# Reading four of the 32 float64 weight pieces through the expert weights' pool

## The chip, the cores and the metric

One NeuronCore of one Trainium2 chip runs the whole program. The metric is the time of one execution on the device in microseconds (us). The engines named below are TensorE (PE, matmuls; PEld is its weight load), VectorE (DVE), ScalarE (ACT), GpSimd (POOL) and SyncE (SP), which here only issues DMA transfers.

## What is computed

Block-local attention gives 1536 tokens of 512 features. A router assigns every token to one of 8 experts (192 tokens each), and each expert is a two-layer MLP in float32. Its output goes through one last MLP whose weights come in float64:

```python
def _moe_ref(x, w_gate, w1, w2):
    ...
    for e in range(E):                      # 8 experts, 192 tokens each
        mask = assigned == e
        h = np.maximum(x[mask] @ w1[e], 0.0)      # 512 -> 1024
        out[mask] = h @ w2[e]                     # 1024 -> 512
    return out.astype(np.float32)

def _moe2_ref(x, w_in, w_out):
    h = x @ w_in                                  # 512 -> 2048, w_in float64
    r = np.maximum(h, 0.0)
    g = r * r
    return (g @ w_out).astype(np.float32)         # 2048 -> 512, w_out float64
```

## The kernel before, in words

Three stages follow each other: attention and its routing scores, then the eight experts (with the rest of the routing woven in), then the last MLP. All instructions are issued in an order that the Python code fixes; each engine runs its own list in order.

**Experts.** Expert `ph` reads four tiles of 128x4x512 floats (1 MB, two DMA transfers each) from a pool `m_w` of eight buffers that are used in turn: tiles 0 and 1 are w1, tiles 2 and 3 are w2. `w_next` keeps a list `wl` of the tiles still to be read and reads the next when the buffer eight places back in the order will be free. SP issues them (L925); before each it loads the expert's number from `ei`, and for tile 1 also a flag `fl` that is set behind the gathers of the tokens. TensorE's matmuls are those of L956 (first layer, 64 for an expert) and L973 (second layer, 64). ScalarE takes the first layer's results out of PSUM (`ht`, L961), ScalarE and VectorE those of the second (`yhi` L979, `ylo` L980).

**Conversion of the float64 weights.** The two matrices are cut into 32 pieces of 128x512 doubles (512 KB). Piece i belongs to quarter i//8; the first four pieces of a quarter are rows of `w_in`, the last four rows of `w_out`. A piece is read into a tile `raw` of the pool `m_stg`, which has two buffers, by `conv_load` (SP, L625). `conv_stream` then turns it into two float32r tiles, the rounded value and the remainder, in four VectorE instructions (L640, L644 and L650 build the float32 bits; L647 subtracts the rounded value of the piece before) and one copy on ScalarE (L643). One call of `conv_step` is one VectorE instruction, so a piece is four steps, 128 in all. Quarter 0 goes to tiles `w2a`, quarter 1 to `w2b`, quarters 2 and 3 to buffers of the expert pool `m_w` that are free by then. The two `raw` buffers alternate: piece i+2 is read when L650 of piece i is done.

**What decides when a piece is converted.** While the experts run, `conv_idle` is called after every piece of TensorE work. It keeps estimated clocks of the engines and issues conversion steps where VectorE is estimated to be idle and the piece is estimated to have landed. In the last MLP a fixed number takes over: six steps after each unit.

**The last MLP.** There are 48 units (3 groups of 512 tokens, 16 blocks of 128 hidden features). A *hidden unit* `hmm(i)` is 12 matmuls of L1065; ScalarE applies the relu (L1068), VectorE squares it (L1069), ScalarE rounds it (L1073) and VectorE makes the remainder (L1074). An *output unit* `omm(i)` is 12 matmuls of L1091 that read both. TensorE's order is hmm(0), hmm(1), hmm(2), omm(0), hmm(3), omm(1) and so on: omm(i) comes after hmm(i+2). Unit i needs quarter (i mod 16)//4 of the weights.

```python
    for i in range(len(seq) + LAG):
        if i < len(seq):
            while ndone[0] < min(len(todo), 8 * (i // 4) + 8):
                conv_step()
            hmm(i)
        if i >= LAG:
            omm(i - LAG)
        conv_step(SF if i < 16 else 1)          # SF = 6
```

Of the kernel before, what the change touches and what calls it, by code (L numbers as in the profile page):

```python
# [9 lines left out]
F32 = mybir.dt.float32  # L10
# [3 lines left out]
I32 = mybir.dt.int32  # L14
# [7 lines left out]
N, DM, E, F, FF = 1536, 512, 8, 1024, 2048  # L22
# [573 lines left out]
def moe(tc, nc, R0, x_dram, m_dram, L9, w1, w2, win, wout, out, identf, identb, dbg=None):  # L596
    ctx = ExitStack()
    const = ctx.enter_context(tc.tile_pool(name="m_const", bufs=1))
    wp = ctx.enter_context(tc.tile_pool(name="m_w", bufs=8))
# [11 lines left out]
    stg = ctx.enter_context(tc.tile_pool(name="m_stg", bufs=2))  # L611
    W, w2b = {}, []
    todo = [(q, io, k) for q in range(4) for io in range(2) for k in range(4)]
    raws = {}

    nload, nfree, eager = [0], [2], [True]

    def conv_load(i):
        q, io, k = todo[i]
        raw = raws[i] = stg.tile([128, 512, 2], I32, name="raw")  # L620
        if io == 0:
            src = win[128 * k:128 * k + 128, 512 * q:512 * q + 512]
        else:
            src = wout[512 * q + 128 * k:512 * q + 128 * k + 128, :]
        nc.sync.dma_start(raw.rearrange("p a b -> p (a b)"), src.bitcast(I32))  # L625
        nload[0] = i + 1

    def conv_stream():

        prev = None  # L630
        for i, (q, io, k) in enumerate(todo):
            if k == 0:
                pool, nm = (w2a, "w2a") if q == 0 else (w2b[0], "w2b") if q == 1 else (wp, "w8")
                W[io, q] = [pool.tile([128, 4, 512], F32R, name=nm) for _ in range(2)]
            while i not in raws:
                conv_load(nload[0])
            raw = raws.pop(i)
            f = stg.tile([128, 512], F32, name="f")
            fi = f.bitcast(I32)
            nc.vector.tensor_scalar(fi, raw[:, :, 1], 3, 0x3FFFFFF8, op0=OP.logical_shift_left, op1=OP.bitwise_and)  # L640
            yield
            if prev:
                nc.scalar.activation(prev[1], prev[0], AF.Copy)  # L643
            nc.vector.scalar_tensor_tensor(fi, raw[:, :, 0], 29, fi, op0=OP.logical_shift_right, op1=OP.bitwise_or)  # L644
            yield
            if prev:
                nc.vector.tensor_tensor(prev[2], prev[0], prev[1].bitcast(F32), op=OP.subtract)  # L647
                ndone[0] = i
                yield
            nc.vector.scalar_tensor_tensor(fi, raw[:, :, 1], -0x40000000, fi, op0=OP.bitwise_and, op1=OP.bitwise_or)  # L650
            nfree[0] = i + 3
            if not eager[0] and i + 2 < len(todo):
                conv_load(i + 2)
            prev = f, W[io, q][0][:, k, :], W[io, q][1][:, k, :]
            yield
        nc.scalar.activation(prev[1], prev[0], AF.Copy)
        nc.vector.tensor_tensor(prev[2], prev[0], prev[1].bitcast(F32), op=OP.subtract)
        ndone[0] = len(todo)

    ndone, nstep, CST = [0], [0], conv_stream()  # L660

    def conv_step(n=1):
        for _ in range(n):
            if w2b or nstep[0] < 32:
                nstep[0] += 1
                next(CST, None)
# [9 lines left out]
    st = {}  # L676
    T = Clock()
# [11 lines left out]
    def routing():  # L689
        tm_at = T.v(0.1)  # L690
        for ph in range(E):
# [70 lines left out]
            else:  # L762
# [10 lines left out]
                T.v(0.4, T.pe + 0.25)  # L773
            d["ei"] = ei
            w_next()

            os_ = rp.tile([128, NBLK], F32, name="os")
# [113 lines left out]
    def t_gather(ph):  # L891

        d = st[ph]
        xa = d["xa"] = f1.tile([128, DM], F32, name="xa")
        xb = d["xb"] = f1.tile([128, DM], F32, name="xb")[0:64, :]
        nc.gpsimd.indirect_dma_start(out=xa, out_offset=None, in_=x_dram,
                                     in_offset=bass.IndirectOffsetOnAxis(ap=sci[:, d["ka"]:d["ka"] + 1], axis=0))
        nc.gpsimd.indirect_dma_start(out=xb, out_offset=None, in_=x_dram,
                                     in_offset=bass.IndirectOffsetOnAxis(ap=d["ib"][:, :1], axis=0))
        fl = d["fl"] = rp.tile([1, 1], I32, name="fl", bufs=4)  # L900
        nc.gpsimd.memset(fl, 0)
        out = T.g(2.3, max(d["ix_at"], T.pe) + 0.1)
        d["tx"] = out + 3.0 + 0.5 * min(max(T.dma - out, 0.0), 3.0)
        T.d(1.0, out)
        w_next()

    wl, done, used = [(ph, i) for ph in range(E) for i in range(4)], [-1], [8]

    def w_next():

        while wl and ("tx" if wl[0][1] else "ei") in st.get(wl[0][0], ()) and 4 * wl[0][0] + wl[0][1] < used[0]:
            w_load(*wl.pop(0))

    def w_load(ph, i):

        d = st[ph]
        eng = nc.sync
        if i == 1:
            eng.value_load(d["fl"][0:1, 0:1], min_val=0, max_val=N - 1)
        r = eng.value_load(d["ei"][0:1, 0:1], min_val=0, max_val=E - 1)  # L920
        s1 = w1[bass.ds(r, 1)].rearrange("o (k p) f -> p (o k) f", p=128)
        s2 = w2[bass.ds(r, 1)].rearrange("o (k p) f -> p (o k) f", p=128)
        t = wp.tile([128, 4, 512], F32, name="w8")
        for k in (0, 2):
            eng.dma_start(t[:, k:k + 2, :], s1[:, k:k + 2, 512 * i:512 * i + 512] if i < 2 else  # L925
                          s2[:, 4 * i - 8 + k:4 * i - 6 + k, :])
        d.setdefault("w", []).append(t)
        T.d(3.1, T.pe)
# [17 lines left out]
    def expert(ph):  # L946
# [3 lines left out]
        for f0 in (0, 2, 4, 6):  # L950
            ps = p_f.tile([128, 2, 256], F32, name="ph", bufs=3)
            for j in range(2):
                f = f0 + j
                w = d["w"][f // 4]
                for k in range(4):
                    nc.tensor.matmul(ps[:, j, 0:CAP], w[:, k, 128 * (f % 4):128 * (f % 4) + 128], d["xt"][:, k, :],  # L956
                                     start=(k == 0), stop=(k == 3), skip_group_check=True)
                    T.p(0.325)
                    if k < 3 or j == 0:
                        yield  # L960
            nc.scalar.activation(d["ht"][:, f0:f0 + 2, :], ps[:, :, 0:CAP], AF.Relu)  # L961
            T.a(0.5, T.pe + 0.2)
            if f0 in (2, 6):
                used[0] += 1
                w_next()
            yield
# [20 lines left out]
    R = routing()  # L987
    nx, ng = [0], [0]
    rt, cur = next(R), None

    freed, landed = {}, {}

    def conv_idle():

        while nload[0] < min(nfree[0], len(todo)) and freed[nload[0]] <= T.pe:
            landed[nload[0]] = T.d(1.6, T.pe) + 2.8
            conv_load(nload[0])
        while (R is None or len(st) >= done[0] + 4) and T.dve < T.pe - 0.3 and landed.get(nfree[0] - 2, 1e9) <= T.pe:
            n0, f0 = nstep[0], nfree[0]
            conv_step()  # L1000
            if nstep[0] == n0:
                return
            T.v(0.7, T.pe - 0.7)
            if nfree[0] > f0:
                freed[nfree[0] - 1] = T.dve + 1.0

    for i in range(2):
        landed[i] = 5.0
        conv_load(i)
    while done[0] < E - 1:  # L1010
        gathers()
        ways = []
# [12 lines left out]
        if way == 0:  # L1025
            rt = next(R, None)
            if rt is None:
                R = None
# [15 lines left out]
            w2b.append(ctx.enter_context(tc.tile_pool(name="m_w2b", bufs=4, side="right", reuse_waits="tile")))  # L1044
        conv_idle()
    eager[0] = False
    while nload[0] < min(nfree[0], len(todo)):
        conv_load(nload[0])
    p_g = ctx.enter_context(tc.tile_pool(name="m_pg", bufs=4, space=PSUM))


# [70 lines left out]
@with_exitstack  # L1122
def kernel(ctx: ExitStack, tc: tile.TileContext, q, k, v, wg, w1, w2, win, wout, out):
    nc = tc.nc
    const = ctx.enter_context(tc.tile_pool(name="const", bufs=1))
    dram = ctx.enter_context(tc.tile_pool(name="dram", bufs=1, space=bass.MemoryType.DRAM))
    identf = const.tile([128, 128], F32, name="identf")
    make_identity(nc, identf)
    identb = const.tile([128, 128], BF, name="identb")
    nc.vector.tensor_copy(identb, identf)  # L1130
    L9 = const.tile([128, NBLK, E + 1], F32, name="L9")
    x_dram = dram.tile([N, DM], F32, name="x_dram")
    m_dram = [dram.tile([N], F32, name=f"m_dram{i}") for i in range(E)]
    ctx.enter_context(tc.manual_schedule())
    route = Route(tc, nc, L9, identf)
    with ExitStack() as actx:
        attention(actx, tc, nc, q, k, v, wg, x_dram, L9, identf, identb, route)
    moe(tc, nc, route, x_dram, m_dram, L9, w1, w2, win, wout, out, identf, identb)
# [29 lines left out]
```

## Time and profile before

| | us |
|---|---|
| median of 3 runs | 592.31 (591.49 to 594.31) |
| the profiled execution | 592.71 |
| its span, first to last instruction | 590.5 |
| PE busy | 570.6 (97%) |
| DVE busy | 342.6 (58%) |
| ACT busy | 195.9 (33%) |
| mean granted TensorE clock | 0.994 |

The busy time of PE is modelled from pipelined matmuls, so 97% does not mean that there is no time to be had in 3%: a matmul at half clock is busy too. The stages are: attention up to about 84 us, experts and routing up to 312, the last MLP from 312.3 to the end. Rows of a timeline give the start and the duration of an instruction and, in brackets, the idle time of its engine before it and what ended that idle time.

### The profile page before, as it was taken

What the parts mean: (1) busy time and instruction counts of PE and PEld (TensorE: products, weight loads), DVE (VectorE), ACT (ScalarE), POOL (GpSimd) and SP (SyncE); (2) the same over time, 40 slices, a digit from 0 to 9 for tenths busy, and PEclk for the clock granted to TensorE, in tenths of its full rate; (3) what the DMA queues carried; (4) which work ended last, traced back from release to release, by engine and by line L of the source; (5) the groups of instructions that cost most, each with busy time, mean ns of one, the idle gap of its engine ahead of it and who ended that gap; (6) DMA issues with size and microseconds to landing.
All of it is one profiled execution on the core that took longest, in us unless ns stands there. A gap on an engine that the chain in (4) does not pass through costs nothing.

```text
span 590.5 us, 10523 instructions
## 1 busy us (share of the span) xinstructions
PE 570.6 (97%) x4131; PEld 475.8 (81%) x4131; DVE 342.6 (58%) x773; ACT 195.9 (33%) x421; POOL 81.2 (14%) x136
## 2 busy tenths in 40 slices
PE   6999998999999999999999998899999999999996
PEld 4777874699898988999998876678888888888884
DVE  5875788887878889634656777772322222322222
ACT  4887862241331314022223333232322222222221
POOL 6663301110401202110000000000300000300002
PEclk9999999999999999999999999899999999999999
DMA  8997224645185474598342433410100000100001
GB/s 223 263 193 142 70 75 143 240 156 193 64 285 202 137 284 140 202 360 309 108 142 73 148 137 108 147 67 2 71 2 0 1 0 1 71 1 0 1 0 71
DMA packets 55392, 71.33 MB, mean 121 GB/s; under 512 B 21296, under 2 KB 32560, under 8 KB 55344
## 3 DMA queue, kind: packets, MB, share of 16 engines
q1 hardware_dynamic: 53360, 64.38, 34.7%
q0 software_dynamic: 1984, 6.29, 3.2%
q8 instruction: 32, 0.52, 0.4%
q14 instruction: 16, 0.13, 0.1%
HBM read 64.37 MB, written 6.29 MB: 120 GB/s over the span
## 4 chain that ended last, share of the span: by engine, by line
PE 65%; issue 14%; DVE 10%; DMA 6%; ACT 2%; POOL 2%; SPq 0%; POOLq 0%; DVEq 0%; ACTq 0%
PE ph L956 15%; PE ph L973 14%; PE pg L1065 9%; PE ph L1091 7%; PE px L1091 2%; PE cnt L582 2%; PE O L284 2%; DMA raw<-in_moe_w_out_dram 2%; PE S L250 2%; PE T L270 2%; DMA raw<-in_moe_w_in_dram 2%; DVE G L570 2%; PE T L193 1%; DVE f L650 1%; DMA rawq<-in_q_dram 1%
## 5 line engine op out<-in xcount | busy, mean ns | idle before, releaser
L956 PE MATMUL ph<-xt,w 128*128 128x192 f32 x512 | 91.1, 331 | 0.0
L973 PE MATMUL ph<-ht,w 128*128 128x192 f32 x512 | 89.3, 329 | 0.0
L570 DVE TENSOR_SCALAR G<-mrow,m 128x1536 bf16<-128x1536 f32 (+4 forms) x108 | 84.9, 839 | 7.5 <-PE cnt L582 3.9
L973 PEld LDWEIGHTS ph<-ht,w 128*128 128x128 f32 x512 | 82.9, 190 | 3.1 <-issue 2.9
L956 PEld LDWEIGHTS ph<-xt,w 128*128 128x128 f32 x512 | 82.5, 190 | 3.4 <-issue 2.7
L1065 PE MATMUL pg<-yhi,w 128*128 128x512 f32 x192 | 59.8, 392 | 2.1 <-ACT w L643 1.6
L1069 DVE TENSOR_TENSOR xa<-xa 128x512 f32<-128x512 f32 x24 | 16.6, 690 | 56.0 <-ACT xa L1068 56.0
L1104 POOL DMA_INDIRECT out_dram<-f,sci x6 | 5.9, 979 | 313.3 <-DVE f L1102 312.6
L1069 DVE TENSOR_TENSOR xb<-xb 128x512 f32<-128x512 f32 x24 | 16.6, 690 | 53.6 <-ACT xb L1068 53.6
L1065 PEld LDWEIGHTS pg<-yhi,w 128*128 128x128 f32 x192 | 36.1, 188 | 10.3 <-ACT w L643 2.0
L1091 PE MATMUL ph<-w,xt 128*128 128x512 f32 x144 | 36.7, 399 | 1.1 <-ACT xt L1073 0.9
L1065 PE MATMUL pg<-ylo,w 128*128 128x512 f32 x96 | 37.6, 392 | 0.0
L961 ACT ACTIVATE ht<-ph 128x384 f32<-128x384 f32 x32 | 15.7, 491 | 60.2 <-PE ph L956 57.9
L1091 PEld LDWEIGHTS ph<-w,xt 128*128 128x128 f32 x144 | 27.8, 194 | 7.8 <-ACT xt L1073 1.3
L1068 ACT ACTIVATE xa<-pg 128x512 f32<-128x512 f32 x24 | 14.2, 592 | 57.6 <-PE pg L1065 57.6
L1068 ACT ACTIVATE xb<-pg 128x512 f32<-128x512 f32 x24 | 14.2, 592 | 55.0 <-PE pg L1065 55.0
L1065 PE MATMUL pg<-yhi,w2a 128*128 128x512 f32 x96 | 29.7, 391 | 0.0
L1065 PE MATMUL pg<-yhi,w2b 128*128 128x512 f32 x96 | 29.5, 389 | 0.0
L979 ACT ACTIVATE yhi<-ph 128x384 fp32r<-128x384 f32 x16 | 7.8, 490 | 63.1 <-PE ph L973 63.1
L263 ACT ACTIVATE P<-S,nm 128x120 f32<-128x120 f32 x96 | 26.6, 370 | 1.9 <-DVE nm L259 1.8
L640 DVE TENSOR_SCALAR f<-raw 128x512 int32<-128x512 int32 x32 | 13.6, 424 | 16.4 <-DMA raw<-in_moe_w_out_dram 9.4
L644 DVE SCALAR_TENSOR_TENSOR f<-raw,f 128x512 int32<-128x512 int32 x32 | 22.1, 690 | 0.8
(242 smaller groups left out, 980.9 us busy)
## 6 DMA issues: line engine op xcount, KB each, us to landing
w<-in_moe_w_dram SPq DMA_DIRECT2D x64, 512.0 KB, 5.4
raw<-in_moe_w_in_dram SPq DMA_DIRECT2D x16, 512.0 KB, 3.6
raw<-in_moe_w_out_dram SPq DMA_DIRECT2D x16, 512.0 KB, 3.3
vw<-in_v_dram SPq DMA_DIRECT2D x16, 240.0 KB, 6.5
rawk<-in_k_dram SPq DMA_DIRECT2D x8, 384.0 KB, 5.4
rawq<-in_q_dram SPq DMA_DIRECT2D x8, 384.0 KB, 6.5
x_dram<-x SPq DMA_DIRECT2D x10, 256.0 KB, 2.0
vw<-in_v_dram SPq DMA_DIRECT2D x8, 80.0 KB, 5.2
```

The costliest lines, as they stand in the source:

```text
L250: nc.tensor.matmul(ss[hh][64 * par:64 * par + 64, i, :], QT[b, hp][r, 128 * c + 64 * par:128 * c + 64 * par + 64], KW_[b, hp][r, 2 * c + p ...
L263: nc.scalar.activation(P[u][:, hh, i], SS[u][hh][:, i], AF.Exp, bias=NM[u][:, hh, i:i + 1])
L570: self.nc.vector.tensor_scalar(t[:, used:used + w], self.mrow[:, 128 * j0:128 * j1], self.m[:, c:c + 1], CS, op0=OP.is_le, op1=OP.mult)
L640: nc.vector.tensor_scalar(fi, raw[:, :, 1], 3, 0x3FFFFFF8, op0=OP.logical_shift_left, op1=OP.bitwise_and)
L644: nc.vector.scalar_tensor_tensor(fi, raw[:, :, 0], 29, fi, op0=OP.logical_shift_right, op1=OP.bitwise_or)
L956: nc.tensor.matmul(ps[:, j, 0:CAP], w[:, k, 128 * (f % 4):128 * (f % 4) + 128], d["xt"][:, k, :], start=(k == 0), stop=(k == 3), skip_grou ...
L961: nc.scalar.activation(d["ht"][:, f0:f0 + 2, :], ps[:, :, 0:CAP], AF.Relu)
L973: nc.tensor.matmul(ps[:, j, 0:CAP], w[:, f % 4, 128 * dd:128 * dd + 128], d["ht"][:, f, :], start=(f == 0), stop=(f == 7), skip_group_chec ...
L1065: nc.tensor.matmul(ps, a[:, k, fs], b[:, k, js], start=(n == 0), stop=(n == 11))
L1068: nc.scalar.activation(r, ps, AF.Relu)
L1069: nc.vector.tensor_tensor(r, r, r, op=OP.mult)
L1091: nc.tensor.matmul(PO[j][t], a[:, 128 * t:128 * t + 128], b[:, f % 4, :], start=(f == 0 and n == 0), stop=(f == 15 and n == 2))
```

## The change

Pieces 2 to 5 no longer pass through the two `raw` buffers. They are read into two tiles of the expert pool `m_w` (two pieces in each tile), which the list `wl` now has as two further entries, behind tile 1 and behind tile 2 of expert 6. The other 28 pieces (`own`) alternate over the two `raw` buffers as before. The pool's buffers are now counted by tiles read (`nw`) instead of by expert and number, so every expert tile behind the new ones goes to a buffer one or two places further on. The estimate of a landing (`landed`) is made for all pieces at one place, with 2.0 instead of 2.8 us added. `len(st) >= done[0] + 5` asks for what `+ 4` asked for, since `st` has one more entry from the start.

```diff
     raws = {}
-
-    nload, nfree, eager = [0], [2], [True]
-
-    def conv_load(i):
+    own = [i for i in range(len(todo)) if not 2 <= i < 6]
+    landed = {}
+
+    nload, nfree, nconv, eager = [0], [2], [0], [True]
+
+    def conv_read(i, raw):
         q, io, k = todo[i]
-        raw = raws[i] = stg.tile([128, 512, 2], I32, name="raw")
+        raws[i] = raw
...
         nc.sync.dma_start(raw.rearrange("p a b -> p (a b)"), src.bitcast(I32))
-        nload[0] = i + 1
+        landed[i] = T.d(1.6, T.pe) + 2.0
+
+    def conv_load():
+        i = own[nload[0]]
+        nload[0] += 1
+        conv_read(i, stg.tile([128, 512, 2], I32, name="raw"))
...
-            nfree[0] = i + 3
-            if not eager[0] and i + 2 < len(todo):
-                conv_load(i + 2)
+            nconv[0] = i + 1
+            if i in own:
+                nfree[0] += 1
+                if not eager[0] and nload[0] < len(own):
+                    conv_load()
...
+    wl.insert(4 * E - 5, (E, 1))
+    wl.insert(4 * E - 6, (E, 0))
+    nw = [0]
+    st[E] = {"ei": None, "tx": None}
 
     def w_next():
 
-        while wl and ("tx" if wl[0][1] else "ei") in st.get(wl[0][0], ()) and 4 * wl[0][0] + wl[0][1] < used[0]:
+        while wl and ("tx" if wl[0][1] else "ei") in st.get(wl[0][0], ()) and \
+                nw[0] < used[0]:
+            nw[0] += 1
             w_load(*wl.pop(0))
 
     def w_load(ph, i):
 
+        if ph == E:
+            t = wp.tile([128, 4, 512], F32, name="w8").rearrange("p (h a) (b c) -> p h (a b) c", h=2, c=2).bitcast(I32)
+            for h in range(2):
+                conv_read(2 + 2 * i + h, t[:, h])
+            return
...
-        while nload[0] < min(nfree[0], len(todo)) and freed[nload[0]] <= T.pe:
-            landed[nload[0]] = T.d(1.6, T.pe) + 2.8
-            conv_load(nload[0])
-        while (R is None or len(st) >= done[0] + 4) and T.dve < T.pe - 0.3 and landed.get(nfree[0] - 2, 1e9) <= T.pe:
+        while nload[0] < min(nfree[0], len(own)) and freed[nload[0]] <= T.pe:
+            conv_load()
+        while (R is None or len(st) >= done[0] + 5) and T.dve < T.pe - 0.3 and landed.get(nconv[0], 1e9) <= T.pe:
```

What moves: TensorE's and GpSimd's lists are the same row for row. On SP, around the reads for experts 6 and 7, the list of before is this (the transfers whose target is `w_` and a number are halves of expert tiles; the first row is the first tile of expert 7):

```order
L925 DMA w_4050<-in_moe_w_dram 128x2x512
L625 DMA raw<-in_moe_w_in_dram 128x1024 x2
L919 TENSOR_LOAD fl
L919 ISA x2
L920 TENSOR_LOAD ei
...
L925 DMA w_4184<-in_moe_w_dram 128x2x512
L625 DMA raw<-in_moe_w_out_dram 128x1024 x4
L625 DMA raw<-in_moe_w_in_dram 128x1024 x4
```

And the list of the changed kernel at that place (the first row is tile 1 of expert 6):

```order
L945 DMA w_3926<-in_moe_w_dram 128x2x512
L627 DMA w_3940<-in_moe_w_in_dram 128x1024 x2
L940 TENSOR_LOAD ei
L940 ISA x2
L945 DMA w_3952<-in_moe_w_dram 128x2x512
L627 DMA w_4032<-in_moe_w_out_dram 128x1024 x2
L627 DMA raw<-in_moe_w_out_dram 128x1024 x2
L940 TENSOR_LOAD ei
```

Pieces 2 and 3 now stand ahead of tile 2 of expert 6 and pieces 4 and 5 behind it; pieces 6 and 7 follow at once in `raw`, since the pieces that held those buffers before them are now 0 and 1. Behind them come tile 3 of expert 6, tiles 0 and 1 of expert 7, piece 8, tile 2, piece 9, tile 3, and then the pieces alone.

On VectorE, where the experts end and the last MLP begins, the list of before is this (L980 is the last drain of an expert, L1069 and L1074 belong to the hidden units, L640 to L650 to the conversion; the target of L647 tells the quarter):

```order
L980 TENSOR_TENSOR ylo<-ph,yhi 128x2x192
L1069 TENSOR_TENSOR xb<-xb 128x512
L1074 TENSOR_TENSOR xt<-xb,xt 128x512
L644 SCALAR_TENSOR_TENSOR f<-raw,f 128x512
L647 TENSOR_TENSOR w2b<-f,w2b 128x512
L650 SCALAR_TENSOR_TENSOR f<-raw,f 128x512
L640 TENSOR_SCALAR f<-raw 128x512
```

And in the changed kernel:

```order
L1000 TENSOR_TENSOR ylo<-ph,yhi 128x2x192
L1087 TENSOR_TENSOR xb<-xb 128x512
L1092 TENSOR_TENSOR xt<-xb,xt 128x512
L651 SCALAR_TENSOR_TENSOR f<-raw,f 128x512
L654 TENSOR_TENSOR w2b<-f,w2b 128x512
L657 SCALAR_TENSOR_TENSOR f<-raw,f 128x512
L647 TENSOR_SCALAR f<-raw 128x512
L651 SCALAR_TENSOR_TENSOR f<-raw,f 128x512
L654 TENSOR_TENSOR w_4470<-f,w_4469 128x512
```

The rows alternate alike, but the conversion is four pieces further on: the first L647 of the stage finishes piece 11 before and piece 15 (the last of quarter 1) in the changed kernel, where the next one already writes quarter 2. Counted over the whole list, 48 conversion steps stand ahead of the first L1069 before and 64 in the changed kernel; from there six steps stand between one L1069 and the next in both, with two steps more ahead of the ninth (of i = 8) and twelve ahead of the thirteenth before, and with four ahead of the twelfth and none from then on in the changed kernel.

## Rows read from the trace of the kernel before

**Rows 1.** Stretches of TensorE's time: busy us of five engines, granted clock, DMA share, GB/s

```profile
368.00:370.00 2.00, 2.00 (x6) 1.57 (x6) 1.97 (x5) 1.11 (x2) 0.00 (x0) 0.52 0.50 119
382.00:384.00 2.00, 2.00 (x5) 1.61 (x6) 1.07 (x3) 0.00 (x0) 0.00 (x0) 0.50 0.50 176
396.00:400.00 4.00, 3.77 (x16) 2.90 (x17) 2.60 (x5) 2.14 (x4) 0.00 (x0) 1.00 0.00 0
```

**Rows 2.** Timeline of TensorE in the last MLP: start, duration, instruction, [idle before]

```profile
320.61 2.20 PE L1091 MATMUL ph<-w2a,xt 128*128 128x512 f32 x9
326.05 2.20 PE L1091 MATMUL ph<-w2a,xt 128*128 128x512 f32 x9
...
353.94 2.11 PE L1091 MATMUL ph<-w2b,xt 128*128 128x512 f32 x8 [0.23 <-DVE xt L1074]
...
366.76 0.50 PE L1091 MATMUL ph<-w,ht 128*128 128x512 f32 x1 [1.84 <-ACT ht L1073]
367.49 3.32 PE L1091 MATMUL ph<-w,ht 128*128 128x512 f32 x8 [0.23 <-DVE ht L1074]
...
371.71 0.62 PE L1065 MATMUL pg<-yhi,w 128*128 128x512 f32 x2
...
380.96 0.50 PE L1065 MATMUL pg<-yhi,w 128*128 128x512 f32 x1 [1.58 <-ACT w L643]
...
395.96 0.50 PE L1091 MATMUL ph<-w,xt 128*128 128x512 f32 x1 [0.92 <-ACT xt L1073]
...
399.31 0.62 PE L1065 MATMUL pg<-yhi,w 128*128 128x512 f32 x2
```

**Rows 3.** Timeline of VectorE in the last MLP

```profile
316.00 0.69 DVE L1069 TENSOR_TENSOR xb<-xb 128x512 f32<-128x512 f32 x1 [2.32 <-ACT xb L1068]
...
327.63 0.69 DVE L1069 TENSOR_TENSOR xb<-xb 128x512 f32<-128x512 f32 x1
...
329.63 0.69 DVE L644 SCALAR_TENSOR_TENSOR f<-raw,f 128x512 int32<-128x512 int32 x1
...
339.64 0.43 DVE L640 TENSOR_SCALAR f<-raw 128x512 int32<-128x512 int32 x1 [1.59 <-DMA raw<-in_moe_w_in_dram]
339.98 0.68 DVE L1069 TENSOR_TENSOR xb<-xb 128x512 f32<-128x512 f32 x1
...
351.81 0.69 DVE L1069 TENSOR_TENSOR xb<-xb 128x512 f32<-128x512 f32 x1
...
391.36 0.69 DVE L644 SCALAR_TENSOR_TENSOR f<-raw,f 128x512 int32<-128x512 int32 x1
...
394.56 0.68 DVE L1069 TENSOR_TENSOR xb<-xb 128x512 f32<-128x512 f32 x1
```

**Rows 4.** Waits on raw tiles, 316 to 392: VectorE's idle us, times; issue to landing

```profile
  DMA raw<-in_moe_w_in_dram: 4.5, 3
  DMA raw<-in_moe_w_out_dram: 3.8, 4
...
DMA to landing us min/median/max: 3.2/3.6/4.4
```

**Rows 5.** SP's queue in the expert stage: start, us from first to last, issues

```profile
250.04 6.59 SPq L925 DMA_DIRECT2D w<-in_moe_w_dram  x8
256.66 1.77 SPq L625 DMA_DIRECT2D raw<-in_moe_w_in_dram  x2
```

**Rows 6.** Timeline of VectorE in the expert stage

```profile
265.30 0.56 DVE L980 TENSOR_TENSOR ylo<-ph,yhi 128x384 fp32r<-128x384 f32 x1 [8.30 <-ACT yhi L979]
266.90 0.43 DVE L640 TENSOR_SCALAR f<-raw 128x512 int32<-128x512 int32 x1 [1.04 <-DMA raw<-in_moe_w_in_dram]
...
307.92 0.56 DVE L980 TENSOR_TENSOR ylo<-ph,yhi 128x384 fp32r<-128x384 f32 x1 [2.50 <-ACT yhi L979]
```

**Rows 7.** Timeline of ScalarE: an expert's last first-layer result

```profile
281.39 0.49 ACT L961 ACTIVATE ht<-ph 128x384 f32<-128x384 f32 x1 [1.59 <-PE ph L956]
```

**Rows 8.** The chain of work that ended last, expert stage: start, us, what

```profile
281.36 10.40 PE ph L973 x64
291.76 10.40 PE ph L956 x64
302.16 10.40 PE ph L973 x64
```

More of the change, by code (lines that the diff above doesn't have):

```diff
@@ L989, in moe @@
     rt, cur = next(R), None
-    freed, landed = {}, {}
+    freed = {}
     def conv_idle():
-        while nload[0] < min(nfree[0], len(todo)) and freed[nload[0]] <= T.pe:
-            landed[nload[0]] = T.d(1.6, T.pe) + 2.8
-            conv_load(nload[0])
-        while (R is None or len(st) >= done[0] + 4) and T.dve < T.pe - 0.3 and landed.get(nfree[0] - 2, 1e9) <= T.pe:
+        while nload[0] < min(nfree[0], len(own)) and freed[nload[0]] <= T.pe:
+            conv_load()
+        while (R is None or len(st) >= done[0] + 5) and T.dve < T.pe - 0.3 and landed.get(nconv[0], 1e9) <= T.pe:
             n0, f0 = nstep[0], nfree[0]
@@ L1005, in conv_idle @@
                 freed[nfree[0] - 1] = T.dve + 1.0
-    for i in range(2):
-        landed[i] = 5.0
-        conv_load(i)
+    conv_load()
+    conv_load()
     while done[0] < E - 1:
@@ L1046, in moe @@
     eager[0] = False
-    while nload[0] < min(nfree[0], len(todo)):
-        conv_load(nload[0])
+    while nload[0] < min(nfree[0], len(own)):
+        conv_load()
     p_g = ctx.enter_context(tc.tile_pool(name="m_pg", bufs=4, space=PSUM))
```

## The prediction, made before the changed kernel was run

> **What bounds the kernel now.** I read the stages first, then TensorE's timeline in the stage that has gaps, then the engine that TensorE waits for there, and last the stage that the change loads more. In the expert stage the chain of waits is TensorE without a break: 64 matmuls in 10.40 us, one layer behind the other [rows 8]; nothing can be won there, only lost. The last MLP is different. Two output units that TensorE runs without a wait start at 320.61 and 326.05 [rows 2], so a unit (12 matmuls of L1065, 12 of L1091) costs 5.44 us, a matmul 0.227. At that pace hmm(15), which follows omm(12), would begin at 320.61 + 12 x 5.44 + 2.72 = 388.61. It begins at 399.31 [rows 2]: TensorE loses **10.70 us** between 320 and 399. From there on it runs at its pace to the end.
>
> The loss has two parts. TensorE waits for the first operand of omm(8) (366.76), for a converted weight in hmm(12) (380.96) and for omm(12) (395.96), with smaller waits between [rows 2]. And after the first two of these the granted clock is 0.52 and 0.50, half of 2.4 GHz; after the third it is 1.00 [rows 1]. What half clock costs: the 11 matmuls from 367.49 to 371.71 take 4.22 us instead of 11 x 0.227 = 2.50, so 1.7 us, and there are two such stretches, about 3.4 of the 10.7.
>
> What TensorE waits for is VectorE. From one L1069 to the next but one, 327.63 to 339.98, VectorE needs 12.35 us where TensorE needs 10.88 [rows 3]. In those 12.35 are two units of squaring and remainder (2.00 us each, from L1069 at 327.63 to L644 at 329.63, with the wait for ScalarE in it), three pieces of conversion, and one wait of 1.59 us for a piece that has not landed [rows 3]. Without the wait the pair is 10.76 us, about TensorE's own pace. So VectorE falls behind by roughly one such wait in every pair of units. The wait is there because a buffer is read again only when L650 has released it: the load takes 3.2 to 4.4 us [rows 4], and where no unit stands in between, one piece of conversion (6.76/3 = 2.25 us) does not cover it. It is 4.5/3 = 1.50 us for pieces of w_in and 3.8/4 = 0.95 for those of w_out [rows 4].
>
> **What the change does, part by part.** It removes no work: 32 loads, 128 steps and all matmuls stay, and TensorE's list is the same. It gives the expert stage two more buffers of two pieces each, so that 16 of the 80 conversion steps left at 316.00 are done by then. In the last MLP the rhythm remains: six steps a unit, two `raw` buffers, one uncovered wait in each pair.
>
> *Does the expert stage take four pieces more?* VectorE has room: it stands idle 8.30 us ahead of the drain at 265.30, and 2.50 ahead of the one at 307.92 [rows 6]. The transfers have to be there. Before, SP issues four expert tiles from 250.04 on, then pieces 2 and 3 from 256.66 [rows 5], which land only in time for L640 at 266.90 [rows 6]. The changed kernel issues, at the same place, tile 1 of expert 6, pieces 2 and 3, tile 2, pieces 4 and 5, pieces 6 and 7: the same 5 MB in another order. So I take all of them to have landed by about 267, pieces 2 and 3 some 7 us earlier. Behind that, pieces 6 to 16 go through two buffers as before; from 267 to 313 that is 11 pieces in 46 us, 4.2 us each, where one piece in a buffer needs about (3.6 + 2.25)/2 = 2.9. I find cover everywhere and take the cost in this stage as **0**.
>
> *What is pushed back.* Tiles 3 of expert 6 and 0 to 3 of expert 7 take buffers that come free later, the last one when expert 6 ends its first layer at 281.36 [rows 8]. It is tile 3 of expert 7, which is read half a pass into the layer that begins at 302.16 [rows 8]; tile 3 of expert 6, issued behind piece 7, has from about 260 to 281.36. Against that cover of 20 us stands the slowest landing that I see, 10 us for the pieces issued at 256.66 [rows 5, 6]. Cost 0; without that cover a late tile would cost TensorE its lateness, one for one. SP's list also has new waits: pieces 6 to 9 wait for L650 of the pieces that held their buffers, and tiles of experts 6 and 7 are queued behind them. Counted on at 2.25 us a piece from 267, VectorE reaches the last of those L650 (of piece 7) at about 276, so the same 20 us cover them.
>
> *ScalarE* gets four copies more among its drains. A copy that waits for a late piece would hold back the drain behind it; the critical one is the last of a first layer, 281.39 [rows 7], which the second layer needs at once. Ahead of it stands now the copy of piece 7, landed by 267 and converted by about 276. Cost 0.
>
> *The last MLP.* The first L1069 stays at 316.00, since it waits for TensorE and ScalarE [rows 3], and the steps behind it are those of piece 16 instead of 12. Ten units with 60 steps follow: 5 pairs of 10.76 us and the waits for pieces 19, 22, 25, 28 and 31, two of w_in and three of w_out: 53.80 + 2 x 1.50 + 3 x 0.95 = 59.65. So L1069 of unit 10 comes at 375.65. An output unit needs its second operand for its second matmul, 2.13 us behind that L1069 (351.81 [rows 3] to 353.94 [rows 2]), so it can begin no earlier than 1.90 behind it without a loss: omm(10) at 377.55. At full pace it would be due at 320.61 + 54.40 = 375.01. Loss **2.54 us**. Then only four steps are left: from L644 at 391.36 to L1069 at 394.56 they take 3.20 [rows 3], so unit 11 has its L1069 at 375.65 + 2.00 + 3.20 = 380.85, its output unit could start at 382.75, and TensorE comes there at 377.55 + 5.44 = 382.99. VectorE has caught up and nothing more is lost. The weights are no limit: quarter 3's w_in, at which hmm(12) stood at 380.96, is converted some ten microseconds earlier.
>
> The 2.54 us come in three doses by the same sum, 0.88 at omm(6), and 0.83 each at omm(8) and omm(10). The waits at 353.94 and at 395.96 are of that size or larger, and 396 to 400 ran at clock 1.00 [rows 1, 2]; so no half clock is left in the sum.
>
> **Sum.** 10.70 - 2.54 = 8.16 us less. The profiled execution took 592.71 us with a span of 590.5, and it stands 0.40 above the median of 592.31. Off the profiled time that is 584.55, off the median 584.15; I say **584.5**, with a span near 582.3.
>
> Bounds: the one size that I take from few rows is the wait for a landing. If all five were as short as those of w_out (0.95), VectorE would be 1.1 us earlier and the loss 1.4; if all were 1.59 as at 339.64, the loss would be 4.6. With the spread of the runs of before (-0.8 to +2.0 about the median), 582.5 to 587.5.
>
> **Rivals.**
>
> *Half clock stays in one place.* If waits bunch into one long one, as at 366.76, a stretch at half clock follows, 1.7 us: 584.5 + 1.7 = 586.2. For it: VectorE is still the slower engine up to unit 10. Against it: each dose is under the wait at 395.96 that left the clock up. The Trainium skill (TensorE: Matmul & The Clock Gate, "What's actually happening") states that the clock is gated by recent activity and that the period over which this is judged runs freely, so that the same kernel may be caught or spared from run to run. The rows bear out that waits of one kind are spared and of another are not; by that page a dose of 0.9 us could be caught too, which would give this rival's time.
>
> *Fewer than four pieces are gained.* If loads in the expert stage land late and the stage ends two pieces ahead, two more units run at six steps: 2 x (5.97 - 5.44) = 1.1 us more, and the weights of quarter 3 come two pieces later. With one half-clock stretch that is 584.5 + 1.1 + 1.7 = 587.3. For it: the pieces land beside 4 MB of expert weights. Against it: the drain at 307.92 finds VectorE 2.50 us ahead [rows 6].
>
> *Slower: the expert stage breaks.* Piece 7 (or a tile behind it on SP) lands so late that ScalarE's copy holds back the drain at 281.39 or that tile 3 of expert 6 is missing. It decides from a landing of piece 7 at about 279 instead of 267, and each microsecond beyond costs one, with 1.7 for the clock. To eat the 8.16 us it would have to land near 286; over 589.35 only then. Nothing in the rows takes that long.
>
> *VectorE keeps up fully.* If the landings shorten to 3.2 us everywhere, the waits shrink to about half and the loss to nearly 0: 582.0.
>
> **Chances.** Forecast as worked out (582.5 to 585.8) 0.74; half clock stays 0.12; fewer pieces 0.07; slower 0.03; VectorE keeps up 0.04. A measurement of this kernel can tell about 0.5%, 2.96 us, from no change. The forecast, the first rival, the last and most of the second are faster by more than that: 0.94; within 0.5% 0.03; slower 0.03. The range 582.2 to 587.5 leaves out the slower case and the edges of the others.
>
> **What would show it.** Right: TensorE's gaps in 350 to 380 shrink to three of about a microsecond, none behind 383; hmm(15) begins near 391.2; the granted clock is 1.00 throughout the stage; VectorE's first L1069 is at 316.0 and its eleventh near 375.7; its waits for `raw` remain, five of 0.9 to 1.6 us. Wrong: a gap of TensorE between 254 and 312; the first L1069 later than 316.5; a pair of units on VectorE that is not about 12 us.

## The result, and the profile after

The changed kernel took a median of 586.81 us (586.31 to 587.43, four runs) against 592.80 for the kernel before (591.49 to 594.31, four runs): 6.0 us less, a ratio of 0.990 (0.987 to 0.993). The forecast was 584.5 with a range of 582.2 to 587.5. The profiled execution took 586.31 us with a span of 584.1, so 6.4 less than the profiled execution of before (592.71).

In its rows the four conversion instructions are L647, L651, L654 and L657 (L640, L644, L647 and L650 before), the experts' layers L976 and L993, and a hidden unit's squaring and remainder L1087 and L1092.

The chain of waits through the expert stage of the changed kernel (start, us, what) is as closed as before [rows 8]:

```profile
281.96 10.40 PE ph L993 x64
292.37 10.40 PE ph L976 x64
302.76 10.40 PE ph L993 x64
313.17 2.75 PE pg L1083 x12
```

The layers take the same 10.40 us; the last MLP begins 0.61 later than before (313.17; the same row of before is 312.56). The time from the first matmul of expert 5 to the first of the last MLP is the same, 65.06 us. In TensorE's timeline, which puts these starts a little earlier than the chain (312.87 for 313.17), first before and then changed:

```profile
247.20 1.14 PE L956 MATMUL ph<-xt,w 128*128 128x192 f32 x6
312.26 0.76 PE L1065 MATMUL pg<-yhi,w2a 128*128 128x512 f32 x2
```

```profile
247.81 1.14 PE L976 MATMUL ph<-xt,w 128*128 128x192 f32 x6
312.87 0.76 PE L1083 MATMUL pg<-yhi,w2a 128*128 128x512 f32 x2
```

VectorE's timeline in this stage shows the first piece in the expert pool picked up at 258.21, where before piece 2 was waited for until 266.90 [rows 6], and still idle time ahead of the drain that before stood at 307.92:

```profile
258.21 0.43 DVE L647 TENSOR_SCALAR f<-w 128x512 int32<-128x512 int32 x1 [0.61 <-DMA w<-in_moe_w_in_dram]
265.17 0.43 DVE L647 TENSOR_SCALAR f<-w 128x512 int32<-128x512 int32 x1 [2.33 <-DMA w<-in_moe_w_out_dram]
284.21 0.43 DVE L647 TENSOR_SCALAR f<-raw 128x512 int32<-128x512 int32 x1 [2.48 <-DMA raw<-in_moe_w_in_dram]
308.52 0.56 DVE L1000 TENSOR_TENSOR ylo<-ph,yhi 128x384 fp32r<-128x384 f32 x1 [2.85 <-ACT yhi L999]
```

So VectorE waits here for pieces, 2.33 us for piece 4 and 2.48 for piece 9, but TensorE has no gap in this stage. In the last MLP the TensorE timeline of the changed kernel, to be read beside [rows 2], is

```profile
321.18 2.20 PE L1109 MATMUL ph<-w2a,xt 128*128 128x512 f32 x9
...
354.37 0.51 PE L1109 MATMUL ph<-w2b,xt 128*128 128x512 f32 x1 [0.39 <-ACT xt L1091]
...
378.67 0.50 PE L1109 MATMUL ph<-w,xt 128*128 128x512 f32 x1 [0.83 <-ACT xt L1091]
...
390.19 2.20 PE L1109 MATMUL ph<-w,xt 128*128 128x512 f32 x9
```

The last of these rows is omm(12). At 5.44 us a unit it would be due at 321.18 + 65.28 = 386.46, so TensorE loses **3.73 us** where it lost 10.70. The stretches of TensorE's time (columns as in [rows 1]) have no half clock left:

```profile
350.00:382.00 32.00, 30.02 (x126) 23.06 (x125) 23.23 (x41) 10.01 (x18) 0.00 (x0) 1.00 0.34 114
382.00:400.00 18.00, 18.00 (x81) 14.89 (x80) 7.20 (x11) 5.64 (x10) 0.00 (x0) 1.00 0.00 0
```

And VectorE's timeline, with the last of its waits for a piece, followed by the L1069 of unit 10 (in the changed kernel L1087), and then the sum of its waits:

```profile
316.56 0.69 DVE L1087 TENSOR_TENSOR xb<-xb 128x512 f32<-128x512 f32 x1 [2.28 <-ACT xb L1086]
...
328.39 0.43 DVE L647 TENSOR_SCALAR f<-raw 128x512 int32<-128x512 int32 x1 [1.41 <-DMA raw<-in_moe_w_in_dram]
...
376.93 0.43 DVE L647 TENSOR_SCALAR f<-raw 128x512 int32<-128x512 int32 x1 [1.78 <-DMA raw<-in_moe_w_out_dram]
377.27 0.69 DVE L1087 TENSOR_TENSOR xb<-xb 128x512 f32<-128x512 f32 x1
```

```profile
  DMA raw<-in_moe_w_out_dram: 3.9, 3
  DMA raw<-in_moe_w_in_dram: 3.1, 2
```

There are five waits, for the pieces that the sum named, 6.9 us in all (1.41, 1.08, 1.64, 1.02 and 1.78). What is left of the loss is VectorE falling behind by one such wait in each pair of units until the conversion ends.

### The profile page after: what moved, and what is told of

Its sections match the earlier page's. It is cut to its first block, busy times and chain, and to the rows that moved or that the text cites. A ratio compares the mean times of both kernels' runs of the same rounds, so it can differ in the third digit from the quotient of the medians.

```text
span 584.1 us, 10522 instructions
## 1 busy us (share of the span) xinstructions
PE 567.4 (97%) x4131; PEld 473.9 (81%) x4131; DVE 343.8 (59%) x773; ACT 196.3 (34%) x421; POOL 83.0 (14%) x136
## 4 chain that ended last, share of the span: by engine, by line
PE 66%; issue 15%; DVE 9%; DMA 6%; ACT 2%; POOL 1%; POOLq 0%; SPq 0%; DVEq 0%; ACTq 0%
PE ph L976 14%; PE ph L993 14%; PE pg L1083 10%; PE ph L1109 8%; PE px L1109 3%; PE O L284 2%; PE cnt L582 2%; PE S L250 2%; PE T L270 2%; DMA raw<-in_moe_w_out_dram 2%; DVE G L570 2%; PE T L193 1%; POOL out_dram L1122 1%; DMA raw<-in_moe_w_in_dram 1%; PE ms L534 1%
## 5 line engine op out<-in xcount | busy, mean ns | idle before, releaser
L976 PE MATMUL ph<-xt,w 128*128 128x192 f32 x512 | 91.1, 331 | 0.0
L993 PE MATMUL ph<-ht,w 128*128 128x192 f32 x512 | 89.3, 329 | 0.0
L993 PEld LDWEIGHTS ph<-ht,w 128*128 128x128 f32 x512 | 82.9, 190 | 3.1 <-issue 2.9
L976 PEld LDWEIGHTS ph<-xt,w 128*128 128x128 f32 x512 | 82.6, 190 | 3.4 <-issue 2.7
L1087 DVE TENSOR_TENSOR xa<-xa 128x512 f32<-128x512 f32 x24 | 16.6, 691 | 57.0 <-ACT xa L1086 57.0
L1087 DVE TENSOR_TENSOR xb<-xb 128x512 f32<-128x512 f32 x24 | 16.6, 691 | 56.1 <-ACT xb L1086 56.1
L905 POOL DMA_INDIRECT xa<-x_dram,sci x8 | 13.4, 1672 | 69.4 <-DVE sci L893 43.5
L1083 PEld LDWEIGHTS pg<-yhi,w2b 128*128 128x128 f32 x96 | 18.0, 188 | 3.8
```

The source lines that it names most:

```text
L993: nc.tensor.matmul(ps[:, j, 0:CAP], w[:, f % 4, 128 * dd:128 * dd + 128], d["ht"][:, f, :], start=(f == 0), stop=(f == 7), skip_group_chec ...
L1083: nc.tensor.matmul(ps, a[:, k, fs], b[:, k, js], start=(n == 0), stop=(n == 11))
L1087: nc.vector.tensor_tensor(r, r, r, op=OP.mult)
```

## The experiments

Two theories were set against each other. **Theory A**: what makes VectorE slower than TensorE is the landing of pieces that no unit covers, one in each pair of units, and, where the conversion is behind, the steps that are made up in one go ahead of units 8 and 12. **Theory B**: VectorE's own work sets the pace, and only pieces converted earlier help. Theory A can be put as a rule for the list: the load of piece i begins behind L650 of piece i-2, so it is waited for unless a unit (2.0 us of VectorE) stands between that L650 and L640 of piece i. Counted on the list of before that marks pieces 15, 18, 21, 24, 26, 29 and 31, as many as VectorE waits for there [rows 4]; on the changed list 19, 22, 25, 28 and 31, again as many. In the changed list, moving the units by one step against the pieces moves a unit into each of these gaps. In the list of before it does so for the first four only (pieces 15, 18, 21 and 24): the steps made up ahead of unit 8 bring the count back to 98, and from there on that list is the old one.

Each kernel ran in four timed runs. The kernel before ran seven times beside each group of four kernels: its median was 594.18 beside the first group (the changed kernel again, one step more in the changed kernel and in the kernel before, half the change) and 593.45 beside the second. "Loss" is TensorE's loss in the last MLP in the profiled execution, from the start of omm(0) and of hmm(15) as above.

| kernel | steps ahead of the last MLP | waits, us | loss, us | median, us | ratio to before |
|---|---|---|---|---|---|
| before | 48 | 8.3 | 10.70 | 594.18 / 593.45 | |
| changed, again | 64 | 6.5 | 3.32 | 586.44 | 0.987 (0.985 to 0.990) |
| changed, one step more | 64 | 0 | 0.0 | 582.81 | 0.981 (0.978 to 0.985) |
| changed, two steps more | 64 | 6.8 | 4.92 | 586.46 | 0.988 (0.986 to 0.990) |
| changed, five steps a unit | 64 | 0 | 0.0 | 582.51 | 0.981 (0.979 to 0.983) |
| half the change | 56 | 6.5 | 4.11 | 586.27 | 0.988 (0.985 to 0.990) |
| half the change, one step more | 56 | 0.2 | 0.0 | 583.20 | 0.981 (0.979 to 0.983) |
| before, one step more | 48 | 4.1 | 6.84 | 590.10 | 0.993 (0.990 to 0.995) |
| before, five steps a unit | 48 | 3.4 | 8.66 | 590.33 | 0.994 (0.991 to 0.996) |

**The changed kernel again.** No edit.

> The changed kernel once more, as it is. Its first profile showed VectorE's first L1069 at 316.56 us, 0.56 later than the kernel before, though nothing in the lists ahead of 250 us differs. Theory (spread of the stages ahead): another profile puts the start of the last MLP anywhere between 315.5 and 317, the loss of TensorE in the last MLP stays at 3.5 to 4.0 us, time 586.3 to 587.4. Rival (the moved transfers delay the expert stage): the start is again 316.5 or later and a gap of TensorE stands between 250 and 312.

The stage began at 313.88 in this profile, later still, with the expert layers again at 10.40 us and no gap. The loss was 3.32 with waits of 6.5 us. In all ten profiles of this study the time from the first matmul of expert 5 to the first of the last MLP is the same, 65.05 or 65.06 us. So the 0.6 us come from the stages ahead, where the lists are still the same. Nor does the change delay the start as a rule: in the chain it lies between 312.56 and 314.69 in the three profiles with 48 steps, between 310.81 and 313.88 in the seven others. Two of the expectations missed by a little: VectorE's first L1069 came at 317.28 (315.5 to 317 expected), and the loss was under 3.5 to 4.0. Beside the kernel before the median is 7.7 us lower here, where the result had 6.0.

**One step more after the first unit.**

```diff
-        conv_step(SF if i < 16 else 1)
+        conv_step(SF + (i == 0) if i < 16 else 1)
```

> The changed kernel with one more conversion step after the first unit of the last MLP and nothing else: from then on every unit's squaring falls between other steps of a piece. Theory A (what is left of the loss is landings that no unit covers): a load is waited for only where no unit stands between L650 of piece i-2 and L640 of piece i. With the steps 64, 70, 76 ... that is so for pieces 19, 22, 25, 28 and 31, with 64, 71, 77, 83 ... for none. The waits of 6.9 us in all vanish, a pair of units costs VectorE 10.8 us, the loss of TensorE goes from 3.7 to below 0.5 us: 582.3 to 583.2. Theory B (VectorE's own work sets the pace): the waits only move, and one step more costs 0.6 us: 586.5 to 587.5.

582.81 us, as Theory A expected, and no loss at all. A piece of VectorE's timeline shows why: between L650 of one piece (here L657, at 331.43) and L640 of the next but one (here L647, at 336.29) there is now a whole unit of squaring and remainder, and the load is done before it is asked for.

```profile
331.43 0.69 DVE L657 SCALAR_TENSOR_TENSOR f<-raw,f 128x512 int32<-128x512 int32 x1
...
334.30 0.69 DVE L1087 TENSOR_TENSOR xa<-xa 128x512 f32<-128x512 f32 x1
335.68 0.69 DVE L1092 TENSOR_TENSOR xt<-xa,xt 128x512 fp32r<-128x512 f32 x1 [0.70 <-ACT xt L1091]
336.29 0.42 DVE L647 TENSOR_SCALAR f<-raw 128x512 int32<-128x512 int32 x1
```

The loads themselves take what they took, 3.4 us in the middle ([rows 4]: 3.6), and TensorE is busy throughout (the last line is its stretch from 350 to 382, where the changed kernel had 30.02 us):

```profile
DMA to landing us min/median/max: 3.1/3.4/4.3
```

```profile
350.00:382.00 32.00, 32.00 (x143) 26.50 (x142) 25.43 (x43) 12.42 (x23) 0.00 (x0) 1.00 0.30 99
```

**Two steps more.** `SF + 2 * (i == 0)` in the same line.

> The changed kernel with two more conversion steps after the first unit instead of one. Theory A (it is where the units stand between the steps that decides): with 64, 72, 78, 84 ... there are again loads that no unit covers, for pieces 18, 21, 24, 27 and 30, so five waits of 6 to 7 us in all return, TensorE loses 3 to 4.5 us: 586 to 587.5. Rival (any step that is done earlier helps): 582 to 583.5, as with one step.

586.46 us, loss 4.92: the waits are back, which shows that it is not the earlier step but the place of the units that counts.

```profile
  DMA raw<-in_moe_w_in_dram: 4.8, 3
  DMA raw<-in_moe_w_out_dram: 2.0, 2
```

The loss came out a little over the 3 to 4.5 expected. Three of its five waits are for pieces of w_in, among them the longest, 1.82 us.

**The same step in the kernel before.**

> The kernel before with that one step and no other change. Theory A: of its seven waits (pieces 15, 18, 21, 24, 26, 29, 31) the first four vanish. VectorE's first L1069 stays at 316, its ninth comes at about 361 instead of 365.4, the thirteenth at about 389 instead of 394.6, so TensorE loses about 5 us instead of 10.7 and is spared at least one of the two stretches at half clock: 586 to 588, most of what the whole change gave. Theory B (only pieces converted earlier help): no gain, 592 to 593.5.

590.10 us, 4.1 less than before in the same comparison; the expectation of 586 to 588 was too good, as was that of a loss of about 5. The first four waits are gone as expected (two loads that a unit covers were still waited for, 0.2 us each), and up to omm(9) TensorE loses nothing. But then TensorE's timeline shows it at a standstill at hmm(12) and omm(12), and a stretch with clock 0.72 follows the first of these:

```profile
379.02 0.49 PE L1065 MATMUL pg<-yhi,w 128*128 128x512 f32 x1 [1.89 <-ACT w L643]
380.02 0.80 PE L1065 MATMUL pg<-yhi,w 128*128 128x512 f32 x1 [0.51 <-DVE w L647]
394.23 0.49 PE L1091 MATMUL ph<-w,xt 128*128 128x512 f32 x1 [1.17 <-ACT xt L1073]
```

```profile
378.00:384.00 6.00, 4.47 (x12) 3.44 (x13) 4.27 (x9) 2.27 (x4) 0.00 (x0) 0.72 0.52 175
```

So the first four waits are about 4 us of the 10.70 of before. The other 6.84 are not all VectorE's own work, since three of the old waits are still in them (1.60, 1.00 and 1.10). An estimate from the rows: from L1069 of unit 0 (318.13) to that of unit 12 (392.83) VectorE takes 74.70 us, 70.6 without its waits of 4.1. At full pace omm(12) begins 65.28 us behind omm(0), which begins 4.61 behind the first L1069, and it wants its own L1069 1.90 ahead: 68.0. Theory B is thus right about some 2.6 us, pieces that are too many in the time that VectorE has, and the waits make up the rest. The same sum for the kernel before (78.56 from 316.00 to 394.56, 70.2 without its waits of 8.3) gives 2.2 of the 10.70. No run has 48 steps ahead and every load covered, so this split stays an estimate.

**Half the change.** Pieces 2 and 3 alone.

```diff
-    own = [i for i in range(len(todo)) if not 2 <= i < 6]
+    own = [i for i in range(len(todo)) if not 2 <= i < 4]
...
-    wl.insert(4 * E - 5, (E, 1))
```

> Half the change: only pieces 2 and 3 go through one tile of the expert pool; 56 steps are done ahead of the last MLP instead of 64 (48 before). Theory A: the rhythm is that of the changed kernel but lasts two units longer, with one wait in each pair (pieces 17, 20, 23, 26, 29), so the loss of TensorE is that of the changed kernel plus about 1 us, 4 to 5 us: 586.8 to 588.2. Rival (every piece converted earlier is worth the same): half of the 6.4 us, 589.2 to 590.

586.27 us, not to be told from the whole change, 586.44, which ran beside it, and under the 586.8 to 588.2 expected. The loss is 4.11, as expected; TensorE waits as briefly as with both tiles, at omm(8) and omm(10) (the lines of the units stand one lower in this kernel):

```profile
365.12 0.50 PE L1108 MATMUL ph<-w,ht 128*128 128x512 f32 x1 [0.57 <-ACT ht L1090]
...
377.28 0.51 PE L1108 MATMUL ph<-w,xt 128*128 128x512 f32 x1 [0.47 <-ACT xt L1090]
```

**Half the change, one step more.**

> Half the change (pieces 2 and 3 in one tile of the expert pool, 56 steps done ahead of the last MLP) with one more step after the first unit. Theory A: no load is waited for, a pair of units costs VectorE 10.8 us, it keeps TensorE's pace until the last piece at unit 12, and TensorE loses nothing, 582 to 583.5, the same as the whole change with that step. Rival (the second tile is worth something when the waits are gone): 584 to 586.

583.20 us, loss 0: with the waits gone (one of 0.2 us is left), the second tile is worth nothing that can be measured. One tile brings eight steps, two bring sixteen (48, 56, 64), so by that count the shorter estimate of a landing, which the change also makes, adds none; the estimate alone was not run.

**Five steps a unit instead of six**, `SF = 5`, in the changed kernel and in the kernel before.

> The changed kernel with five conversion steps after a unit instead of six. Theory A: no load is left uncovered until unit 11, VectorE gains 0.3 us on TensorE with each unit, and what is left, nine steps ahead of unit 12, fits into that lead: TensorE loses less than 1 us, 582 to 584. Rival (slower conversion makes the weights of quarter 3 late): a gap of TensorE at hmm(12), 585 to 588.

> The kernel before with five steps instead of six, without the change. Theory A adds that VectorE has a fixed amount of work, 80 steps and 12 units from 316 us on (24 + 45 us without a wait), where TensorE would be at omm(12) after 66: what is not done in the rhythm comes as 15 steps ahead of unit 8 and 15 ahead of unit 12, so TensorE stands there, 6 to 10 us in all: 588 to 592.5. Rival (the rhythm alone decides): 582 to 584, as with the change.

The changed kernel took 582.51 us with no loss. VectorE is ahead: at unit 11 it waits for TensorE's result by way of ScalarE, not the other way round.

```profile
368.79 0.69 DVE L657 SCALAR_TENSOR_TENSOR f<-raw,f 128x512 int32<-128x512 int32 x1
369.96 0.69 DVE L1087 TENSOR_TENSOR xa<-xa 128x512 f32<-128x512 f32 x1 [0.48 <-ACT xa L1086]
```

The kernel before took 590.33 us with five steps, and nearly all of its 8.66 us of loss stands in one place, hmm(12), whose weights are not there (idle time in brackets), with a clock of 0.59 from 380 to 388:

```profile
376.63 0.50 PE L1065 MATMUL pg<-yhi,w 128*128 128x512 f32 x1 [0.91 <-DVE w L647]
377.90 0.50 PE L1065 MATMUL pg<-yhi,w 128*128 128x512 f32 x1 [0.53 <-ACT w L643]
381.10 0.80 PE L1065 MATMUL pg<-yhi,w 128*128 128x512 f32 x1 [2.70 <-DVE w L647]
```

```profile
380.00:388.00 8.00, 6.90 (x19) 5.47 (x20) 6.79 (x13) 1.84 (x3) 0.00 (x0) 0.59 0.40 131
```

Here two loads that a unit covers were waited for as well, 0.57 and 0.36 us, so the rule of Theory A names the long waits and not every short one.

In these runs neither pieces converted ahead nor a better rhythm took the loss away alone; both together did. With both, three kernels that lie within 0.7 us of each other beat the changed kernel by 3 to 4 us.

## Why the prediction was right, and where its size was off

*The bound and the mechanism held.* VectorE was what TensorE waited for; the gain came from the last MLP and from nowhere else; the rhythm of six steps and one uncovered wait in each pair remained, with the five waits at the pieces that the sum had named; VectorE caught up behind unit 10, and both stretches at half clock went.

*The half clock was a symptom.* The prediction counts about 3.4 of the 10.70 us as half clock. As a share of TensorE's time that is right, but in the kernel before it cost nothing of its own: between the first L1069 and that of unit 12 VectorE waits for loads and for ScalarE, and nowhere for a matmul, so it would have been as late at omm(12) with TensorE at full clock. Its only wait for a hidden unit's result is that of unit 0:

```profile
DVE xb L1069 <- ACT xb L1068: 2.3, 1, 2.3
```

So the 1.7 us by which the rivals price a stretch at half clock is not a price while VectorE sets the pace. It can be one where TensorE stands at the weights: in the kernel before with five steps, L1069 of unit 12 comes 74.49 us behind the first, 6.5 over the 68.0 of above, and the loss is 8.66; in the 2.2 us between lie the standstill at hmm(12) and the half clock behind it.

*The expert stage cost nothing, as worked out.* The same 65.06 us before and after show it. The landings were tighter than I had them: I took pieces 2 to 7 to be there by about 267 and the slowest landing to be 10 us. Pieces 6 and 7, issued at 256.3 and 257.6, took 11.2 and 11.1 us, so they came up to 2 us later, still ahead of their conversion at 272.18 and 274.47; of those behind, piece 8 was waited for 1.64 us and piece 9 2.48, up to 284.21. The idle time ahead of the drain at 308.52 shows that the cover was there all the same, 2.85 us.

*The term that was mis-sized is the wait for a landing.* The sum had 5.85 us; measured were 6.9, and L1069 of unit 10 came 60.71 us behind that of unit 0 instead of 59.65; the five pairs without the waits took 53.8, as in the sum. I had taken two prices, one for each matrix, from seven waits. The waits for w_out do not keep to one price: the one for piece 31 was 1.78 us, in the second profile 1.60, where before it was 0.96. That is 1.06 of the 1.19 us by which the loss, 3.73, is over 2.54; the other 0.13 are not assigned. The bound of 1.59 did not hold for each wait (1.64 and 1.78 are over it), but five waits at it make 7.95 us, and the loss stayed under the 4.6 that they gave.

*The remaining 0.6 us are no step of the change.* 584.55 + 1.19 + 0.61 for the later start of the stage is 586.35; the profiled execution took 586.31. It was the fastest of the four; the median, 586.81, is another 0.5 above it. The start of the last MLP varied from 310.81 to 314.69 over the profiles, with the same lists up to about 250 us. A sum made against one execution has that uncertainty in it, more than I gave it. For the same reason one sign that was to show the prediction wrong did come, a first L1069 later than 316.5 (316.56, and 317.28 in the second profile): the limit was set inside that spread. And 586.81 lies above the 582.5 to 585.8 to which the prediction gave 0.74; it is in the whole range only, so the size was met less well than the mechanism.

*The rivals.* "Half clock stays in one place" did not come about: the longest wait, 0.83 us at 378.67, left the clock at 1.00, and that the median is near this rival's 586.2 is chance. The longer standstills of the kernels with 48 steps (1.58 us and more in one bracket) each went with a lower clock, and none of the waits of about a microsecond that stood alone did (1.17 at 394.23 in the kernel before with one step more, 0.83 here, 0.57 and 0.47 in half the change). The Trainium skill (TensorE: Matmul & The Clock Gate, "What's actually happening") has the clock follow how busy the engine has been recently, and so far the traces agree. That the same wait is caught in one execution and spared in another, as the prediction drew from it, no run here shows. "VectorE keeps up fully" gave the right time for what happens then, 582.0, but the wrong way to it: the landings need not become shorter, they need a unit in front of them.

*What the prediction did not see* is that the four pieces are worth no more than two, since it asked what the change gives and not what the least of it would give. By the same sum half the change has one pair of units more at the slower pace, 0.8 to 1.4 us; the loss shows 0.4 to 0.8 (4.11 against 3.73 and 3.32), and the times of the two kernels show nothing.

## What to carry to other kernels

Where two buffers alternate between a load and an engine, do not ask only whether the engine has enough work for the load on the average: look in its list at what stands between the release of a buffer and its next use, since a load that is covered in two of three places is still waited for in the third, every time round. Shifting the interleaving by one instruction was worth 4.1 us in the kernel before and 3.6 on top of the change, with no work added, where the change itself was worth 6.0 and 7.7. And before more work is moved ahead, work out when the slower engine catches up: here the last two of the four pieces done early bought nothing that can be measured.

## What the runs showed of the hardware that was not expected

The start of the last MLP spread by 3.9 us over ten profiles, from 310.81 to 314.69, while the 65 us right ahead of it repeated to a hundredth. The spread stems from the attention and the first experts with their routing, whose lists are the same in all kernels. A comparison of two profiles by their spans alone would have been misleading: the execution of "two steps more" that was profiled took 585.16 us, less than that of the changed kernel, although it lost 1.2 us more in the stage in question; its stage began 2.4 us earlier.

Why the landing of piece 31 took longer in the changed kernel is left open. Between 366 and 377 us only the loads of two pieces and one small transfer of the instruction queue ran there:

```profile
q1 hardware_dynamic: 294, 1.05, 30.4%
q8 instruction: 1, 0.02, 0.8%
```

In the kernel before there was no such transfer beside that piece, but no run here tells whether it is the cause.
